# A weight load issued from ScalarE ahead of the opening barrier, in a kernel whose time is its DMA traffic

## The chip, the cores and the metric

One core of one Trainium2 chip. The metric is device time in microseconds (us), median of several executions. Before: 1271.49 us, six runs between 1271.37 and 1271.73. The profile comes from one execution; its span (1269.6 us before) is some 2 us shorter than the timed figure. Times inside an execution count from the span's start.

## The reference

```python
# A_k_cache, A_v_cache: 2 x 8 x 32768 x 256 bf16, 537 MB together; x: 2 x 448; wq: 448 x 4096
g = _sigmoid((x * gate_w).sum(-1, keepdims=True))
q = x @ wq                                   # 16 heads of 256, two to a K/V head
scores = einsum(q, k) * 256 ** -0.5;  p = softmax(scores);  a = (p @ v) @ wo
h = gelu(x @ w1 + b1);  b = h @ w2 + b2
return g * a + (1 - g) * b
```

(Shortened to its shapes.) One decode step for two sequences: little arithmetic, 547 MB to read once.

## The kernel before

A ring of three slots in SBUF takes tiles of K and V of 8.39 MB (64 KB on each of 128 partitions). SyncE issues them in the order K0, WQ, W1, K1, K2, V0, K3, V1, K4, V2 and so on; a tile may be issued once its slot's last user is done. WQ and W1 share a slot, and K2 takes it over. V0 goes where K0 was, V1 where K2 was.

```python
def first_load(E):                    # SyncE, placed ahead of the opening barrier
    s0 = slot_of[("K", 0)]
    E.ins(lambda e: e.dma_start(cut(s0, 0, SLOT), kv_src(A_k_cache, 0)), key=("fill", ("K", 0)), stream=f"slot{s0}")

def prog_sp(E):                       # SyncE, behind the barrier
    for d in order[1:]:
        for pd in before_of[d]:
            E.wait("pe", released(pd))
        kind, idx = d
        if kind == "WQ":
            parts = [(wq_f, A_wq[0:KC * P, :]...), (wq_r, A_wq[KC * P:Dm, :]...)]   # 3072 KB and 512 KB
            for i, (o, src, _) in enumerate(parts):
                dma(lambda e, o=o, src=src: e.dma_start(o, src), "slot0", ("wq", i))
        ...                           # W1, then the tiles of K and V

def prog_act(E):                      # ScalarE, behind the barrier
    dma(lambda e: e.dma_start(x_sb, A_x[:, 0, :]), "d_x", "x")
    for b in range(Bn):
        dma(...gate_w..., "d_gw", ("gw", b))
    ...                               # the biases b1 and b2; then compute

def prog_dve(E):                      # VectorE, cut to the opening
    E.wait_total("d_x");  ...         # xm: x for the last rows of WQ
    E.wait_total("d_gw"); ...         # gate product, sum; waits for an exponential of ScalarE; omg, dg
    K(0)                              # four transposes of K0
    E.wait_total("d_b");  ...         # copies b2_f, g32, omB
    gelu1()                           # waits for HW (x @ w1 on TensorE), copies h, first half of the gelu
    gelu2(); K(1); ...
```

TensorE projects Q from x and WQ, computes x @ w1 (its end is "HW"), waits for VectorE's copy of h, then computes the scores S(K0), S(K1) and so on. S(K0) releases K0's slot for V0.

## Time and profile before

| | before |
|---|---|
| median, six runs | 1271.49 us |
| bytes read, mean rate | 547.43 MB, 431 GB/s |
| busiest compute engine | TensorE, 55% of the span |
| SyncE's DMA queue | 99.8% of the 16 DMA engines' time |

The lines, and how they are read, are in the prediction below.

### The profile page before, as it was taken

How to read it: one execution, taken by the hardware profiler on the slowest of the kernel's cores; microseconds unless marked ns; L12 is line 12 of the kernel's file. 1: busy time of each engine (PE TensorE's matmuls, PEld its weight loads, DVE VectorE, ACT ScalarE, POOL GpSimd, SP SyncE). 2: the span in 40 equal slices, each digit the busy share in tenths (PEclk: the TensorE clock that was granted, in tenths of full speed). 3: DMA queues.
4: the chain of work that ended last, by engine and by line, in shares of the span. 5: the costliest groups of instructions: out<-in, count | busy, mean ns of one | idle time of the engine just before them, and what ended most of it. 6: DMA issues, size and time to landing. Idle time of an engine off the chain costs nothing.

```text
span 1269.6 us, 7458 instructions
## 1 busy us (share of the span) xinstructions
PE 699.4 (55%) x4386; PEld 141.0 (11%) x1842; DVE 690.0 (54%) x311; ACT 44.7 (4%) x184; POOL 4.4 (0%) x19
## 2 busy tenths in 40 slices
PE   0977457635466554665544665444664546655365
PEld 0211001100011110111000111000110001111012
DVE  4676536655365563556735467453755636557351
ACT  0100000000000000000000000000000000000000
POOL 1000000000000000000000000000000000000000
PEclk9888787776788677877767877778877678877787
DMA  9999999999999999999999999999999999999998
GB/s 407 451 429 428 432 432 432 447 432 428 429 432 434 438 432 440 434 432 429 432 429 442 432 436 438 432 429 429 432 442 432 434 440 432 429 429 432 442 424 371
DMA packets 11114, 547.58 MB, mean 431 GB/s; under 512 B 1368, under 2 KB 1632, under 8 KB 2144
## 3 DMA queue, kind: packets, MB, share of 16 engines
q1 hardware_dynamic: 10948, 547.43, 99.8%
q8 instruction: 7, 0.11, 0.0%
q10 hardware_dynamic: 156, 0.01, 0.0%
q14 instruction: 3, 0.02, 0.0%
HBM read 547.43 MB, written 0.00 MB: 431 GB/s over the span
## 4 chain that ended last, share of the span: by engine, by line
DMA 61%; PE 19%; DVE 14%; issue 5%; SPq 0%; ACT 0%; ACTq 0%
DMA ring<-in_A_k_cache_dram 57%; DVE ring L758 12%; PE ps_s L525 6%; PE ps_s L342 6%; PE ps_o L342 4%; DMA ring<-in_A_wo_dram 3%; DVE mx L762 1%; DMA PT<-in_gate_w_dram 1%; PE ps_o L574 1%; PE ps_m L539 0%; PE ps_m L534 0%; DVE gmax L764 0%; PE ps_o L468 0%; DVE gmx L768 0%; PE ps_o L439 0%
## 5 line engine op out<-in xcount | busy, mean ns | idle before, releaser
L758 DVE STREAM_TRANSPOSE ring<-ring 128x4096 uint32<-128x4096 uint32 x128 | 557.6, 4413 | 379.8 <-DMA ring<-in_A_k_cache_dram 379.6
L525 PE MATMUL ps_s<-ring,Abd 128*128 128x512 bf16 x1024 | 424.9, 415 | 399.9 <-DVE ring L758 399.4
L342 PE MATMUL ps_s<-ring,Abd 128*128 128x512 bf16 x1024 | 421.2, 411 | 0.0
L525 PEld LDWEIGHTS ps_s<-ring,Abd 128*128 128x128 bf16 x1024 | 105.7, 103 | 819.3 <-DVE ring L758 462.0
L342 PE MATMUL ps_o<-ring,PT 128*24 128x512 bf16 x1504 | 114.0, 411 | 0.0
L544 PE MATMUL ps_f<-o_sb,selg 128*32 128x257 f32 x32 | 17.0, 634 | 91.1 <-DVE o_sb L791 89.9
L574 PE MATMUL ps_o<-ring,PT 128*24 128x512 bf16 x544 | 57.9, 424 | 12.8 <-DMA ring<-in_A_v_cache_dram 12.8
L762 DVE TENSOR_REDUCE mx<-ps_s 128x1 f32<-128x1024 f32 x16 | 19.6, 1225 | 62.8 <-PE ps_s L342 62.8
L675 ACT ACTIVATE negm<-ps_m 128x1 f32<-128x1 f32 x16 | 2.7, 171 | 1131.8 <-PE ps_m L539 1131.8
L775 DVE STREAM_TRANSPOSE PT<-pexp 128x1024 bf16<-128x1024 bf16 x16 | 19.9, 1244 | 39.7 <-PE ps_o L342 39.7
L791 DVE TENSOR_REDUCE o_sb<-ps_o 128x256 f32<-128x2048 f32 x15 | 34.4, 2291 | 0.5
L789 DVE TENSOR_TENSOR ps_o<-ps_o,mask 128x2048 f32<-128x2048 f32 x15 | 34.3, 2290 | 0.0
L574 PEld LDWEIGHTS ps_o<-ring,PT 128*24 128x24 bf16 x544 | 14.7, 99 | 104.8 <-issue 87.9
L772 DVE COPY ls<-lsum 128x1 f32<-128x1 f32 x16 | 2.5, 154 | 32.1 <-ACT pexp L679 32.1
L669 ACT COPY Abd<-qrep 32x16 bf16 (+1 forms) x128 | 19.5, 199 | 0.6
L679 ACT ACTIVATE pexp<-ps_s,negm 128x1024 bf16<-128x1024 f32 x16 | 17.8, 1114 | 1.7
L534 PE MATMUL ps_m<-ident_f,mx 128*1 128x128 f32 x32 | 6.1, 271 | 21.1 <-DVE mx L762 21.1
L439 PE MATMUL ps_o<-ring,xT 128*32 128x512 bf16 x16 | 6.2, 608 | 20.5 <-issue 20.5
L544 PEld LDWEIGHTS ps_f<-o_sb,selg 128*32 128x32 f32 x32 | 2.9, 140 | 109.5 <-DVE o_sb L791 107.4
L539 PE MATMUL ps_m<-ones_f,gmx 1*128 1x1 f32 x32 | 6.4, 267 | 9.9 <-DVE gmx L768 9.9
L805 DVE TENSOR_SCALAR o_sb<-ps_o,mask 128x256 f32<-128x256 f32 x1 | 0.5, 484 | 15.6 <-PE ps_o L342 15.6
L764 DVE TENSOR_REDUCE gmax<-ps_m 1x2 f32<-1x128 f32 x16 | 4.4, 278 | 7.5 <-PE ps_m L534 7.5
(87 smaller groups left out, 78.0 us busy)
## 6 DMA issues: line engine op xcount, KB each, us to landing
ring<-in_A_v_cache_dram SPq DMA_DIRECT2D x1, 4096.0 KB, 27.2
ring<-in_A_v_cache_dram SPq DMA_DIRECT2D x2, 2048.0 KB, 34.0
ring<-in_A_wq_dram SPq DMA_DIRECT2D x1, 3072.0 KB, 28.6
ring<-in_B_w_dram SPq DMA_DIRECT2D x1, 1568.0 KB, 32.9
ring<-in_A_wo_dram SPq DMA_DIRECT2D x1, 1568.0 KB, 36.2
ring<-in_B_w_dram SPq DMA_DIRECT2D x1, 1344.0 KB, 32.2
ring<-in_A_wo_dram SPq DMA_DIRECT2D x1, 1008.0 KB, 38.2
ring<-in_A_wo_dram SPq DMA_DIRECT2D x1, 560.0 KB, 39.1
```

Source lines behind the costliest of these rows:

```text
L342: return e.add_instruction(mybir.InstMatmult(name=f"I-{nc.next_id()}", engine=mybir.EngineType.PE, ldweights=False, ins=[e.lower_ap(x), e. ...
L525: fn = lambda e, o=o, x=x, st=st, sp=sp, s=s, w=w: e.matmul(o, a_win(s, w), x, start=st, stop=sp, skip_group_check=True)
L539: E.ins(lambda e: e.matmul(ps_m[:, C_BC:C_BC + 1], gmx[:, :], ones_f[0:1, 0:1], start=True, stop=True), key=("M2", g))
L544: E.ins(lambda e: e.matmul(ps_oa, selg[:, :], o_sb[:, :], start=False, stop=False, skip_group_check=True), key=("OT", g))
L574: fn = lambda e, o=o, x=x, wt=wt, st=st, sp=sp, j=j: e.matmul(o, wt, x, start=st, stop=sp, skip_group_check=True)
L669: E.ins(lambda e, o=o, Q=Q, c=c: e.copy(o[:, :, c:c + 2], qrep[32 * Q:32 * Q + 32, :, bass.ds(E.dyn(2 * g, 2), 2)]), key=(("A", g) if (Q = ...
L679: E.ins(lambda e: e.activation(pexp[:, :].rearrange("p (r i a) -> p i r a", r=CR, i=2), ps_s[:, :].rearrange("p (i r a) -> p i r a", i=2, ...
L758: E.ins(lambda e: e.transpose(k_words(idx, blk), k_words(idx, blk)), key=("T", idx, blk))
L762: E.ins(lambda e: e.tensor_reduce(mx[:, :], ps_s[:, :], AX.X, ALU.max), key=("MX", g))
L775: E.ins(lambda e: e.transpose(PT[:, :], pexp[:, :]), key=("PT", g))
L789: E.ins(lambda e: e.tensor_tensor(p, p, mb, ALU.mult), key=("OM", g))
L791: E.ins(lambda e: e.tensor_reduce(o_sb[:, 0:Dh], ps_o[:, :].rearrange("p (n d) -> p d n", d=Dh), AX.X, ALU.add), key=("OS", g))
```

## The change

Its intent: start WQ at once, beside the first K tile, from a sequencer that is free at that moment, so that the Q projection isn't kept waiting behind 8.39 MB of K.

```diff
+        def second_load(E):
+            E.ins(lambda e: e.dma_start(wq_f, A_wq[0:KC * P, :].rearrange("(p k) n -> p (k n)", p=P)), key=("wq", 0),
+                  stream="slot0")
...
-                    for i, (o, src, _) in enumerate(parts):
+                    for i, (o, src, _) in list(enumerate(parts))[1:]:
                         dma(lambda e, o=o, src=src: e.dma_start(o, src), "slot0", ("wq", i))
...
         first_load(engs["sp"])
+        second_load(engs["act"])
...                                  # and both loads are moved ahead of their engine's part of the barrier
```

More of the change, by code (lines that the diff above doesn't have):

```diff
@@ L857, in bass_gated_mix__gqa_block_cached__dense_activation_gelu__decode_kernel @@
         entry = nc.main_func.blocks[-1]
-        n0 = len(entry.instructions)
-        engs["sp"].eng = nc.sync
-        first_load(engs["sp"])
-        ins = entry.instructions
-        at = next(i for i, x in enumerate(ins) if x.engine == mybir.EngineType.SP and type(x).__name__ == "InstDrain")
-        entry.instructions = ins[:at] + ins[n0:] + ins[at:n0]
+        for nm, eng, kind, load in (("sp", nc.sync, mybir.EngineType.SP, first_load),
+                                    ("act", nc.scalar, mybir.EngineType.Activation, second_load)):
+            n0 = len(entry.instructions)
+            engs[nm].eng = eng
+            load(engs[nm])
+            ins = entry.instructions
+            at = next(i for i, x in enumerate(ins) if x.engine == kind and type(x).__name__ == "InstDrain")
+            entry.instructions = ins[:at] + ins[n0:] + ins[at:n0]
         with nc.Block("main") as block:
```

## The prediction

> **What bounds the kernel now.** I read the page first: the busy shares, the table of DMA queues, the mean rate.
>
> ```profile
> PE 699.4 (55%) x4386; PEld 141.0 (11%) x1842; DVE 690.0 (54%) x311; ACT 44.7 (4%) x184; POOL 4.4 (0%) x19
> ...
> q1 hardware_dynamic: 10948, 547.43, 99.8%
> ...
> q10 hardware_dynamic: 156, 0.01, 0.0%
> ...
> HBM read 547.43 MB, written 0.00 MB: 431 GB/s over the span
> ```
>
> No compute engine is busy for more than 55% of the span, but the packets of queue q1 (SyncE's: it holds all the large loads) fill 99.8% of the 16 DMA engines' time. q10 is ScalarE's, with 156 small packets. The view by stretches shows whether that rate has headroom:
>
> ```profile
> 0.00:73.00 73.00, 40.26 (x187) 11.08 (x121) 42.82 (x37) 5.64 (x15) 4.42 (x19) 0.93 1.01 431
> ...
> 100.00:1200.00 1100.00, 598.91 (x3760) 114.49 (x1457) 601.58 (x240) 34.88 (x154) 0.00 (x0) 0.77 1.00 433
> ```
>
> The last two columns are DMA share and GB/s: share 1.00 at 433 GB/s through the middle. The time is bytes over rate plus the two ends. A microsecond in which the DMA engines have no work is lost for good; time that compute gains is worth nothing unless the engines run dry. So the question is how close the opening comes to running dry, and that is read from the timeline (start, duration, engine, line, what; in brackets the idle time before and what ended it):
>
> ```profile
> 0.00 0.40 SPq L374 DMA_DIRECT2D ring<-in_A_k_cache_dram  x1
> ...
> 0.80 0.55 ACTq L637 DMA_DIRECT2D pexp<-in_A_x_dram  x1
> 0.81 0.80 SPq L388 DMA_DIRECT2D ring<-in_A_wq_dram  x2
> ...
> 9.59 0.29 DVE L716 COPY xm<-pexp 2x64 bf16<-2x64 bf16 x2 [5.34 <-DMA pexp<-in_A_x_dram]
> ...
> 19.28 0.61 DVE L718 TENSOR_TENSOR gp_sb<-pexp,PT 2x448 f32<-2x448 bf16 x1 [9.39 <-DMA PT<-in_gate_w_dram]
> ...
> 22.17 17.42 DVE L758 STREAM_TRANSPOSE ring<-ring 128x4096 uint32<-128x4096 uint32 x4 [0.62 <-DMA ring<-in_A_k_cache_dram]
> 30.79 0.10 PEld L439 LDWEIGHTS ps_o<-ring,xT 128*32 128x32 bf16 x1 [20.57 <-issue]
> ...
> 45.82 0.69 DVE L732 COPY PT<-ps_o 128x512 f32<-128x512 f32 x1 [5.13 <-PE ps_o L473]
> ...
> 65.35 0.33 SPq L410 DMA_DIRECT2D ring<-in_A_v_cache_dram  x1
> 79.22 0.33 SPq L410 DMA_DIRECT2D ring<-in_A_k_cache_dram  x1
> 106.07 0.33 SPq L410 DMA_DIRECT2D ring<-in_A_v_cache_dram  x1
> 113.19 17.42 DVE L758 STREAM_TRANSPOSE ring<-ring 128x4096 uint32<-128x4096 uint32 x4 [10.88 <-DMA ring<-in_A_k_cache_dram]
> ```
>
> The reader sees four things. WQ (the large part is 24 KB on each of 128 partitions) already waits in the queue at 0.81 us while the first K tile is still moving, so the DMA engines never wait for its issue. x and gate_w, a few KB behind nothing on their own queue, still land only at 9.59 and 19.28 us. The Q projection starts at 30.8 us, when WQ is in. And V0, K3 and V1 are issued at 65.35, 79.22 and 106.07 us, each when its ring slot has been used.
>
> **What the Trainium skill says.** "DMA: Bandwidth & Descriptors", section "Issuing engines are not separate DMA queues": loads from ScalarE and SyncE run on the same 16 engines and interleave; issuing from two saves only sequencer time. Here that is the 0.80 us at L388, under 20 us of queued K. Same page, "Queues, rings and completion order": each DMA engine takes turns between the rows it has work for, packet by packet, and consumes one row in order. The trace agrees in a way I lean on: 433 GB/s over 16 engines is 27.1 GB/s, so one 64 KB packet of K takes 2.42 us. The first packets start at 1.64 us. Three packets end at 8.9 and seven at 18.6; x and gate_w are used 0.7 us after those two moments. The packet counts fit if a data packet and its semaphore packet are each one turn (q10: 4 for x, 4 for gate_w, 144 for b1, 4 for b2 make 156). Same page, "Where 436 GB/s comes from": a fabric ceiling of 435 GB/s. 433 sits at it, so I give a second queue no extra bandwidth.
>
> **The change, part by part.**
>
> Bytes: none added or removed. Issue: SyncE loses one of the two issues in 0.80 us, ScalarE gains one at 0.00, under the barrier that SyncE's own 0.40 us issue holds anyway. Start of data: still 1.64 us. Gain 0.
>
> Order of data: each engine has 8 K packets (2.42 us) and 8 WQ packets (24 KB: 0.91 us). Taking turns, a pair takes 3.33 us, and eight pairs end at 1.64 + 26.6 = 28.3 us. WQ's large part lands with K0 at some 29.4 (K0 before: drained at 1.64 + 8 x 2.42 = 21.0, seen at 22.17, so 1.15 for landing). K0 therefore lands 7 us later and WQ about as before, for its remainder still follows K0 on SyncE's queue.
>
> What moves without being in the diff: **x, gate_w and the biases are now behind WQ on ScalarE's row**. They start at 28.4 us. Their turns are now against 4 KB packets of the WQ remainder (0.15 us), so x should be usable near 29.7 and gate_w near 30.3, instead of 9.6 and 19.3.
>
> The chain from there. xm at 29.7, x transposed by TensorE, the table load (1.28 us) and the copy of xT (0.17): before, 9.59 to 11.86, so 2.3 us, to 32.0. The Q projection starts at 32.0 instead of 30.8: +1.2. It and what follows end with HW, at 45.8 before, at 47.0 now. On VectorE: gate product and sum 1.3 us, the exponential after xT (32.2), four small operations 0.75, so the transposes of K0 start at 33.0 instead of 22.17 and end at 50.4 instead of 39.6. Only behind them come the copies b2_f, g32, omB (0.65) and the copy of h, at 51.1 instead of 45.82. So 5.3 us of the 10.8 reach TensorE: S(K0) starts at 54.2 instead of 48.9. It takes 16.45 us before (48.9 to 65.35), part of it at half clock; I keep that.
>
> From S(K0) everything is a chain without gaps: V0's issue at 65.35 + 5.3 = 70.7; S(K1) back to back, K3's at 84.5; softmax, then the transposes of K2 (they started at 84.89, right behind the transposed P), then S(K2): V1's at 106.07 + 5.3 = 111.4.
>
> When does the queue run dry? K3 landed at 113.15, so drained at 112.0 after 1.15 for landing. One 8.39 MB tile takes 19.36 us: V0 ahead of it drained at 92.6, K2 at 73.3. With 1.64 us from issue to first packet, the deadlines are 71.7 for V0, 91 for K3, 110.4 for V1. Slack before: 6.3, 11.7 and 4.3 us. Against a delay of 5.3: V0 holds by 1.0, K3 easily, **V1 misses by 1.0 us**. V2 was issued at 134.35 with 15 us queued ahead of it, so the loss happens once and isn't repeated. Sum: 1271.5 + 0 (issue) + 0 (bytes) + 0.9 (the expected shortfall, rounded for clock luck) = 1272.4 us.
>
> **The rivals.**
>
> Hidden altogether: if x and gate_w land a bit earlier, or the half-clock stretch (PEclk 0.5 from 48 to 53 us) falls in the new idle time of TensorE (47 to 51) instead of in S(K0), the delay is under 4.3 us and nothing starves: 1271.4. For: the slack is of the size of the delay. Against: idle time has gone with a low clock here, not cured it.
>
> A real bubble: the small loads land later than I say (their 8 data packets of b1 and the semaphores take turns with the 10 KB packets of W1), or S(K0) and S(K1) meet a longer half-clock stretch. Every 1 us more is 1 us more, at V0 and V1 alike: 1274 to 1276.
>
> A gain: WQ early lets the Q projection start early, or two queues fill the engines better at the start. For the first nothing speaks, as it still waits for the WQ remainder and x, both late; and earlier compute doesn't move a DMA bound. For the second: the stretch to 73 us already averages 431 GB/s with the start in it. At most some tenths: 1271.0.
>
> **Range and chances.** The centre is 1272.4. Low end 1270.9: no bubble and a few tenths saved. High end 1275.2: delay of 8 us instead of 5.3. A verdict of faster or slower needs 25 us; the largest loss I can construct from the opening is under 10, and steady state, with 15 us and more queued, absorbs the rest. So same 0.98.
>
> **What would show it.** Right: x's copy at VectorE and the Q projection at 29 to 32 us; the K0 transposes at 33; b2_f's copy after 50; V0, K3 and V1 issued about 5 us later; the middle still at 433 GB/s and share 1.00; from the second group on every event later by the same constant, the change in time. q10 at about 3.15 MB and 300 packets (156 + 128 + 16). Wrong: if x lands near 10 us the two rows do not work as I read them and nothing is lost; if K0 still lands at 22 us the rows don't share turn by turn; if V1's delay exceeds 6 us without a bubble my deadlines are off; if the time falls by over 1 us there was something at the start that I took for fixed.

## The result, and the profile after

After: 1273.69 us, median of six runs between 1273.22 and 1274.92. Ratio to before 1.0019, 95% interval 1.0006 to 1.0032: 2.2 us slower, which counts as the same at 2%, but the two sets of runs don't overlap. (Here and below a ratio is the mean time of one kernel's fast runs over that of the other's of the same rounds, so not quite the ratio of the medians quoted.)

From the page of the changed kernel, TensorE's and VectorE's busy time and the two DMA queues:

```profile
PE 704.5 (55%) x4386; PEld 141.6 (11%) x1842; DVE 689.7 (54%) x311; ACT 44.7 (4%) x184; POOL 4.4 (0%) x19
...
q1 hardware_dynamic: 10804, 544.28, 99.1%
q10 hardware_dynamic: 300, 3.15, 0.6%
```

q10, ScalarE's queue, now holds 3.15 MB and 300 packets: the 156 from before, 128 rows of WQ and 16 semaphore packets. The bytes have moved, and no other part of the DMA traffic has grown. Next the timeline of the changed kernel's opening (start, duration, engine, line, what; in brackets the idle time before and what ended it):

```profile
0.00 0.41 SPq L374 DMA_DIRECT2D ring<-in_A_k_cache_dram  x1
0.12 0.40 ACTq L377 DMA_DIRECT2D ring<-in_A_wq_dram  x1
0.94 0.50 ACTq L641 DMA_DIRECT2D pexp<-in_A_x_dram  x1
...
29.66 0.29 DVE L720 COPY xm<-pexp 2x64 bf16<-2x64 bf16 x2 [25.27 <-DMA pexp<-in_A_x_dram]
30.26 0.61 DVE L722 TENSOR_TENSOR gp_sb<-pexp,PT 2x448 f32<-2x448 bf16 x1 [0.30 <-DMA PT<-in_gate_w_dram]
31.97 0.61 PE L443 MATMUL ps_o<-ring,xT 128*32 128x512 bf16 x1 [1.60 <-ACT xT L650]
32.72 17.40 DVE L762 STREAM_TRANSPOSE ring<-ring 128x4096 uint32<-128x4096 uint32 x4
50.63 0.69 DVE L736 COPY PT<-ps_o 128x512 f32<-128x512 f32 x1
54.02 0.61 PE L529 MATMUL ps_s<-ring,Abd 128*128 128x512 bf16 x1
70.33 0.33 SPq L414 DMA_DIRECT2D ring<-in_A_v_cache_dram  x1
84.20 0.33 SPq L414 DMA_DIRECT2D ring<-in_A_k_cache_dram  x1
111.02 0.33 SPq L414 DMA_DIRECT2D ring<-in_A_v_cache_dram  x1
113.46 17.43 DVE L762 STREAM_TRANSPOSE ring<-ring 128x4096 uint32<-128x4096 uint32 x4 [6.16 <-DMA ring<-in_A_k_cache_dram]
153.53 17.43 DVE L762 STREAM_TRANSPOSE ring<-ring 128x4096 uint32<-128x4096 uint32 x4 [5.01 <-DMA ring<-in_A_k_cache_dram]
```

WQ is issued 0.7 us sooner and the Q projection begins 1.2 us later, at 31.97 instead of 30.8, because x, issued behind WQ on the same queue, is first used at 29.66. The same two points in the kernel before, S(K0)'s start and the arrival of K4, are:

```profile
48.90 0.61 PE L525 MATMUL ps_s<-ring,Abd 128*128 128x512 bf16 x1
...
151.90 17.42 DVE L758 STREAM_TRANSPOSE ring<-ring 128x4096 uint32<-128x4096 uint32 x4 [5.39 <-DMA ring<-in_A_k_cache_dram]
```

S(K0) is 5.1 us later. K3 arrives 0.27 us later than before (113.46 against 113.19), but K4, which follows V1, arrives 1.63 us later. Between those two lies V1, issued at 111.02 instead of 106.07. Stretches around that moment show the hole, first before, then after. The last two columns are DMA share and GB/s; a packet of 2.4 us is counted where it starts, so only an empty stretch among full ones means something:

```profile
110.50:111.75 1.25, 0.00 (x0) 0.00 (x0) 0.00 (x0) 0.00 (x0) 0.00 (x0) 1.00 1.70 734
111.75:112.75 1.00, 0.00 (x0) 0.00 (x0) 0.00 (x0) 0.00 (x0) 0.00 (x0) 0.52 0.30 131
```

```profile
110.50:111.75 1.25, 1.25 (x19) 0.20 (x8) 0.00 (x0) 0.00 (x0) 0.00 (x0) 1.00 0.01 0
111.75:112.75 1.00, 1.00 (x25) 0.10 (x4) 0.00 (x0) 0.00 (x0) 0.00 (x0) 1.00 2.61 918
```

Before, most engines start their first packet of V1 at about 111, right behind the last one of K3. After, no K or V packet starts between 110.50 and 111.75; V1 starts at 112.0, one microsecond after its issue. The DMA records in the trace, put together engine by engine (each packet joined to the one that ended just ahead of it), show 14 of the 16 engines with a gap of 0.5 to 2.1 us there (mean 1.14), and none before; the other two were busy with K3 until 112.7 and 113.0. The first packet behind the gap takes 3.0 us on average instead of 2.42. The wider stretches confirm it, before and then after:

```profile
80.00:120.00 40.00, 23.27 (x138) 4.70 (x56) 26.47 (x11) 2.49 (x11) 0.00 (x0) 0.77 0.98 423
120.00:200.00 80.00, 43.80 (x270) 8.40 (x105) 45.17 (x19) 2.49 (x11) 0.00 (x0) 0.78 1.00 433
```

```profile
80.00:120.00 40.00, 27.15 (x157) 5.32 (x63) 26.99 (x11) 2.48 (x11) 0.00 (x0) 0.83 0.95 407
120.00:200.00 80.00, 44.38 (x266) 8.53 (x104) 43.82 (x18) 2.50 (x11) 0.00 (x0) 0.76 1.01 434
```

From 80 to 120 us the rate is 407 GB/s against 423: 16 GB/s over 40 us is 0.64 MB, 1.5 us at 433 GB/s. From 120 us on the rates agree.

### The profile page after: what moved, and what is told of

Its sections match the earlier page's. It is cut to its first block, busy times and chain, and to the rows that moved or that the text cites. A ratio compares the mean times of both kernels' runs of the same rounds, so it can differ in the third digit from the quotient of the medians.

```text
span 1271.5 us, 7458 instructions
## 1 busy us (share of the span) xinstructions
PE 704.5 (55%) x4386; PEld 141.6 (11%) x1842; DVE 689.7 (54%) x311; ACT 44.7 (4%) x184; POOL 4.4 (0%) x19
## 3 DMA queue, kind: packets, MB, share of 16 engines
q10 hardware_dynamic: 300, 3.15, 0.6%
## 4 chain that ended last, share of the span: by engine, by line
DMA 62%; PE 20%; DVE 14%; issue 3%; SPq 0%; ACT 0%; DVEq 0%; ACTq 0%
DMA ring<-in_A_k_cache_dram 57%; DVE ring L762 12%; PE ps_s L529 7%; PE ps_s L342 7%; PE ps_o L342 4%; DMA ring<-in_A_wo_dram 3%; DMA pexp<-in_A_x_dram 2%; DVE mx L766 1%; PE ps_o L578 1%; PE ps_m L543 0%; PE ps_m L538 0%; DVE gmax L768 0%; DVE gmx L772 0%; PE ps_m L483 0%; SPq L404 0%
## 6 DMA issues: line engine op xcount, KB each, us to landing
ring<-in_A_wq_dram ACTq DMA_DIRECT2D x1, 3072.0 KB, 29.4
```

## The experiments

**The theory:** on ScalarE's queue x and gate_w stand behind WQ, VectorE's gate chain and with it K0's transposes start late, h is copied behind them, S(K0) starts 5 us late, V1 is issued after the DMA engines have run out of work, and those empty microseconds stay in the time. **The rivals:** two queues that share the engines cost rate by themselves; issuing ahead of the barrier costs something; the delay of the compute is hidden, and the loss is elsewhere.

Five timed runs of each kernel, with nine of the kernel before in each group (1271.49 us in the first, 1271.54 in the second). All gave correct results.

### x and gate_w ahead of WQ

```diff
         def second_load(E):
+            (x, then the two rows of gate_w: moved here from the start of ScalarE's program)
             E.ins(lambda e: e.dma_start(wq_f, ...
```

> The changed kernel with x and gate_w issued by ScalarE ahead of WQ (all ahead of the barrier). Theory (the loss comes from x and gate_w standing behind WQ on ScalarE's row, which holds up the K0 transposes and with them V1's issue past its deadline): x near 10 us and gate_w near 20 us, K0 landing still near 29 us for it shares with WQ, transposes of K0 from 29.5, S(K0) from about 50.8 instead of 54.0, V1 issued near 108, no dry stretch: 1271.4 to 1271.9 us. Rival (two rows sharing the DMA engines cost rate, wherever x stands): still 1273 to 1274 us.

Measured: 1271.48 us (1271.41 to 1271.61), ratio 1.0. From its timeline:

```profile
7.27 0.30 DVE L721 COPY xm<-pexp 2x64 bf16<-2x64 bf16 x2 [1.75 <-DMA pexp<-in_A_x_dram]
16.84 0.61 DVE L723 TENSOR_TENSOR gp_sb<-pexp,PT 2x448 f32<-2x448 bf16 x1 [9.27 <-DMA PT<-in_gate_w_dram]
28.37 17.42 DVE L763 STREAM_TRANSPOSE ring<-ring 128x4096 uint32<-128x4096 uint32 x4 [9.25 <-DMA ring<-in_A_k_cache_dram]
...
106.90 0.33 SPq L418 DMA_DIRECT2D ring<-in_A_v_cache_dram  x1
```

WQ still shares the engines with K0, and K0 lands at 28.37 instead of 22.17. That alone costs nothing: S(K0) starts at 48.85 (I had expected 50.8), as before. In the kernel before VectorE stands idle for 5.13 us until HW, and that takes up the delay of the transposes but for 0.47 us: h is copied at 46.29 instead of 45.82. So sharing is not the cause. Nor is it a gain: the Q projection starts at 30.69 us, as before.

### WQ behind the barrier, still ahead of x

```diff
-        second_load(engs["act"])            # and its move ahead of the barrier
 def prog_act(E):
+    second_load(E)                          # on a semaphore of its own, which TensorE also waits for
     dma(lambda e: e.dma_start(x_sb, ...
```

> WQ issued by ScalarE behind the barrier, still ahead of x (on a semaphore of its own). Theory: the barrier has nothing to do with it, x and gate_w are still behind WQ: everything as in the changed kernel, x near 29.7, V1 near 111, 1273 to 1275 us. Rival (issuing ahead of the barrier delays the start or the barrier): back to 1271.5 us.

Measured: 1273.58 us (1273.10 to 1275.26), ratio 1.0019; x used at 29.48, V1 issued at 111.41. The loss is all there without the early issue. The barrier is not part of it; the order on the queue is.

### The copy of h ahead of K0's last transpose

```diff
-            K(0)
+            for blk in range(3):
+                T(0, blk)
 ...
             gelu1()
+            T(0, 3)
             gelu2()
```

> The changed kernel with VectorE's copy of h and the first half of the gelu moved ahead of the fourth transpose of K0; the loads are those of the changed kernel. Theory (late x hurts only through VectorE's order, h behind four transposes): x still near 29.7 and transposes from 32.7, but h copied near 46.5 instead of 50.6, S(K0) from about 50 instead of 54, V1 issued near 107, no dry stretch: 1271.4 to 1271.9 us. Rival (sharing itself costs rate): 1273 to 1274 us.

Measured: 1271.53 us (1271.43 to 1271.80), ratio 1.0. Its timeline:

```profile
29.49 0.29 DVE L720 COPY xm<-pexp 2x64 bf16<-2x64 bf16 x2 [25.09 <-DMA pexp<-in_A_x_dram]
...
32.55 13.08 DVE L762 STREAM_TRANSPOSE ring<-ring 128x4096 uint32<-128x4096 uint32 x3
45.56 0.34 DVE L831 CAST gp_sb<-PT 2x448 f32<-2x448 bf16 x1
46.14 0.69 DVE L736 COPY PT<-ps_o 128x512 f32<-128x512 f32 x1
...
104.75 0.33 SPq L414 DMA_DIRECT2D ring<-in_A_v_cache_dram  x1
```

The loads are those of the changed kernel and x is as late as there, but h is copied at 46.14 instead of 50.63 and V1 is issued at 104.75. The loss is gone. In this kernel a late x hurts only through VectorE's program order.

### x late, and WQ left where it was

```diff
 def prog_act(E):                            # the kernel before
+    E.wait(f"slot{slot_of[('K', 0)]}", ("fill", ("K", 0)))
     dma(lambda e: e.dma_start(x_sb, ...
```

> The kernel before, WQ on SyncE's queue as it was, but ScalarE waits for K0 to land before it issues x, gate_w and the biases. Theory: lateness of x and gate_w alone makes the loss: gate_w near 30 us, transposes of K0 from about 32, S(K0) from about 53.5, V1 issued near 110.5, 1272.3 to 1273.7 us. Rival (the loss needs two rows sharing the engines): 1271.5 us although x is late.

Measured: 1273.22 us (1271.90 to 1274.64), ratio 1.0017; gate_w used at 29.22, transposes of K0 from 31.41, V1 issued at 109.89. The loss appears with all large loads on one queue. The executions scatter widely, and the profiled one (span 1270.1) is at their fast end. Still, the interval of the ratio, 1.0003 to 1.0031, lies above 1.

### Delay alone

The last four kernels touch no load. They add 6, 12 or 18 dummy memsets, each waiting for the last, to VectorE just ahead of the copy of h:

```diff
+                for i in range(6):                      # or 12, 18
+                    if i:
+                        E.wait("dve", f"zz{i - 1}")
+                    E.ins(lambda e: e.memset(ps_o[:, 1536:2048], 0.0), key=f"zz{i}")
                 E.ins(lambda e: e.tensor_copy(h_sb[:, :], ps_o[:, 1024:1536]), key="hr")
```

> The kernel before with 6 chained dummy memsets (about 0.5 us each) on VectorE just ahead of the copy of h: S(K0) and all that hangs on it about 3 us later, no load touched. Theory (a late V1 costs only beyond a deadline that the runs so far put at 109.6 to 109.9 us): V1 near 109.2, at the edge: 1271.4 to 1272.2 us. Rival (any delay of the opening shows in the end): 1274.5 us.

> The same with 12 memsets, about 6 us. Theory: V1 near 112.3, some 2.6 us past its deadline, plus a few tenths for the restart: 1273.7 to 1275.2 us, though all loads are issued as in the kernel before. Rival (delay of the compute is hidden, and the loss of the changed kernel came from its loads): 1271.5 us.

> The same with 18 memsets, about 9 us. Theory: beyond the deadline one microsecond of delay is one microsecond of time, whether V0 or V1 takes it: 3 us above the run with 12, 1276.5 to 1278.5 us. Rival (the loss saturates, since later tiles have queue in hand): within 1 us of the run with 12.

> The changed kernel with 6 memsets, about 3 us more on top of its own 5. Theory: it is past the deadline already, so all of it shows: 1276.0 to 1277.5 us, where the same 3 us cost the kernel before next to nothing. Rival (the loss of the changed kernel is not V1's deadline): 1273.5 to 1274.5 us.

Measured: 1272.38, 1275.32 and 1280.26 us on the kernel before, 1277.06 us on the changed one. I had the memsets at 0.5 us; with the wait each took 0.67, so the doses were 4, 8 and 12 us (in the profiled executions the copy of h came 3.0, 7.8 and 10.9 us later than in the kernel before) and the figures expected for 6, 12 and 18 memsets are too low by that (1272.2, 1275.2 and 1278.5 were their upper ends). The issue of V0 and V1 with 18 memsets:

```profile
77.00 0.33 SPq L410 DMA_DIRECT2D ring<-in_A_v_cache_dram  x1
...
118.05 0.33 SPq L410 DMA_DIRECT2D ring<-in_A_v_cache_dram  x1
```

Here V0 is too late as well, and not only here. The stretch in which V0's first packets start in the kernel before, and the same stretch with 12 memsets (V0 issued at 72.83):

```profile
72.00:72.60 0.60, 0.60 (x5) 0.10 (x1) 0.56 (x1) 0.00 (x0) 0.00 (x0) 1.00 3.55 1529
72.60:73.70 1.10, 1.10 (x7) 0.28 (x3) 0.00 (x0) 0.00 (x0) 0.00 (x0) 1.00 0.14 60
```

```profile
72.00:72.60 0.60, 0.60 (x4) 0.18 (x2) 0.60 (x1) 0.00 (x0) 0.00 (x0) 1.00 0.01 0
72.60:73.70 1.10, 1.10 (x6) 0.19 (x2) 1.10 (x1) 0.00 (x0) 0.00 (x0) 1.00 0.00 0
```

By the DMA records there is a gap ahead of V0 on 15 engines with 12 memsets (mean 1.6 us), and on all 16 in the changed kernel with 6 memsets (2.4) and with 18 memsets (5.7). K3 then ends later, and V1's deadline moves with it, so that the gaps ahead of V1 are no more than 1.3, 1.3 and 1.8 us in these three. All ten kernels, in the order of V1's issue in their profiled execution (the time is the median of all runs; the profiled execution of "before, x late" itself took 1271.90):

| kernel | V0 issued | V1 issued | median us |
|---|---|---|---|
| changed, h ahead of the last transpose | 64.05 | 104.75 | 1271.53 |
| before | 65.35 | 106.07 | 1271.49 |
| changed, x and gate_w ahead of WQ | 65.84 | 106.90 | 1271.48 |
| before, 6 memsets | 67.60 | 108.30 | 1272.38 |
| before, x late | 69.16 | 109.89 | 1273.22 |
| changed | 70.33 | 111.02 | 1273.69 |
| changed, WQ behind the barrier | 70.55 | 111.41 | 1273.58 |
| before, 12 memsets | 72.83 | 113.52 | 1275.32 |
| changed, 6 memsets | 73.71 | 114.40 | 1277.06 |
| before, 18 memsets | 77.00 | 118.05 | 1280.26 |

Flat up to 106.90, then rising, whatever made V1 late: a late x, another queue or dummy work. From the changed kernel to the last row V0 moves by 6.67 us, V1 by 7.03 and the time by 6.57; in the last three rows more than half of the loss arises at V0, not at V1. The rivals that the delay is hidden, or that the loss saturates, fall. The corner is softer than a deadline: with 6 memsets V1 comes at 108.30, where the engine records show a gap over 0.3 us on only two engines, and the median is already 0.9 us up (but the interval of its ratio, 0.9996 to 1.0023, holds 1). These gaps open more than 2.5 us after V1's issue, so the 1.0 us that V1 takes from issue to first packet doesn't explain them; the cause stays open.

## Why the prediction was right or wrong

The time, 1273.69, lies in the range of 1270.9 to 1275.2 and in the class of 98%. The mechanism was right at each step on the path to V1; one term was too small. Off that path HW was wrong, without effect: it ended 1.7 us earlier than predicted, and VectorE came to h only later.

| step | predicted | measured |
|---|---|---|
| x, gate_w used | 29.7, 30.3 | 29.66, 30.26 |
| Q projection starts | 32.0 | 31.97 |
| HW ends | 47.0 | 45.3 |
| transposes of K0 start | 33.0 | 32.72 |
| h copied | 51.1 | 50.63 |
| S(K0) starts | 54.2 | 54.02 |
| V0, K3, V1 issued | 70.7, 84.5, 111.4 | 70.33, 84.20, 111.02 |
| time added | 0.9 | 2.2 |

**Order of data, turn by turn:** right. 3.33 us for a pair of a K and a WQ packet put x at the right tenth of a microsecond; in the DMA records K and WQ packets do alternate one to one on each engine, and the kernel with x first shows the other side of it: x used at 7.27. K0 was seen to land there at 28.37, 1 us sooner than the 29.4 I had.

**VectorE's order passes on 5.3 of 10.8 us:** right (5.1 of 10.55), and shown by the run that changes only that order.

**No gain from issue, bytes or a second queue:** right. With x out of WQ's way the change is worth 0.0 us.

**"V1 misses by 1.0 us":** this is the term that was mis-sized, by a misreading of when the engines run dry. I took K3 as drained at 112.0, its landing less 1.15 us. By the engine records of the kernel before, half of the engines have ended K3 by 111.15 and the last by 112.71, 0.5 us before the tile is used: most of the 1.15 was the spread between the engines, and each engine that runs dry loses its own time. So the slack was 0.9 us smaller than I had it. The 1.64 us from issue to first packet was misread as well, without harm. K0's first packets start 1.05 to 1.90 us after the issue and take 2.7 to 3.4 us instead of 2.42; V1's start 1.0 us after theirs and take 3.0. About 1.0 us of start and 0.6 us of a slow first packet make up the 1.64, so its sum was right. V1 itself came 0.4 us earlier than I had it. Together: 1.0 + 0.9 - 0.4 = 1.5 us, and by the records the 16 engines end V1 1.5 us later on average (gaps of 1.0 and slow packets of 0.5, spread over all 16).

The rest lies in the slowest engine. K4's arrival, which waits for it, comes 1.63 us later; the last packet of K or V in the whole kernel ends 1.83 us later than before (the average engine's last one: 1.51), and the profiled spans differ by 1.85. Over the ten profiles the change in the span is that of this last packet within 0.03 us, but for the kernel with h ahead of the last transpose (0.2 against 0.4). With 6 memsets it is 0.96 us, where the average engine loses 0.2. Why the slowest engine falls back further than the average isn't settled.

**The scatter:** the changed kernel's runs span 1.7 us, those of before 0.4. This I only argue: S(K0) took between 15.4 us (6 memsets) and 17.0 us (x first) from start to V0's issue in these profiles, and TensorE's clock is at half at its start. The Trainium skill says why that may vary, in "TensorE: Matmul & The Clock Gate", part 1 on the clock gate: the activity window runs freely, so the number of slow matmuls differs from run to run. This trace shows the two rates (0.43 us from matmul to matmul at 54 us, 0.22 at 60); with one profile for each kernel, no run here shows the variation from run to run. While V1 has slack the variation is hidden; past the corner it shows.

## What to carry to other kernels

When a kernel is bound by DMA, ask of a change to the loads not what it starts sooner but what now stands behind it in the same queue, and follow that to the next large issue and to the moment when the engines would run out of work. A few KB that gate the compute go ahead of megabytes on their queue. Slack in an opening is finite and is read per DMA engine, not from the landing of a tile; up to its end a delay is free, and past it each microsecond costs about one, plus a restart.

## What the Trainium skill lacked or had wrong

- "DMA: Bandwidth & Descriptors", section "Issuing engines are not separate DMA queues": it says that issuing from two engines only saves sequencer time. It doesn't draw what follows for small loads, that the choice of queue decides what they stand behind: x was first used at 9.59 us with WQ on the other queue, at 29.66 behind it.
- Same page, "Queues, rings and completion order": it gives a packet as 9 to 17 descriptors typically. It doesn't give the size of a turn in bytes, and the trace doesn't show descriptors. Here a turn was one partition's whole row: 64 KB of K and 24 KB of WQ alternate on each engine (2.42 and 0.91 us). A semaphore write took a turn of its own (x: data at 6.7 us, semaphore at 9.1), so a small load beside rows of 64 KB pays 2.42 us a turn and needs two turns.
- Same page, "Latency and other measured facts": about 0.6 us to the first byte on this path. Here V1's first packets started 1.0 us after its issue began (112.0 against 111.02) and 0.64 us after the 0.33 us of issuing ended, so the figure fits if it counts from the end of the issue; the page doesn't say from where. What I found on no page is the slow restart: the first packet behind a gap took 3.0 us instead of 2.42. With it, V1's late issue cost the engines 1.5 us on average, and 1.0 us of that was the gap itself.
